# Pooled attention and a routed FFN on one core: emission order from a list scheduler, attention in thirds, four weight buffers

## The chip, the cores and the metric

The kernel runs on one core of one Trainium2 chip. A core has five engines with an instruction queue each: TensorE (PE, matmuls into PSUM; its weight loads are listed as PEld), VectorE (DVE), ScalarE (ACT), GpSimd (POOL) and SyncE (SP). Here GpSimd issues all loads,[...] and SyncE issues most stores. The metric is the device time of one execution in microseconds (us).

## The reference

Two parts follow each other. The first is attention over keys and values that are averaged over groups of 8 tokens; the second sends each token to the one of 8 experts whose embedding is nearest by cosine.

```python
batch, heads, seq, dim = 8, 8, 576, 64          # experts: 8, width 512 -> 1024 -> 512
k_p = k.reshape(B, H, 72, 8, D).mean(axis=3);  v_p = likewise
scores = q @ k_p.T / sqrt(D)
attn = exp(scores - max); attn /= sum(attn) + 1e-9
x = (attn @ v_p) as [4608 tokens, 512]
...
logits = normalized(x) @ normalized(expert_emb).T / tau
e = argmax(logits);  gate = softmax(logits)[e]
out = gate * (relu(x @ w1[e]) @ w2[e])
```

Which expert each token takes is known only on the chip, so the weights have to be fetched by a number that the kernel computes itself.

## The kernel before

The work is cut by batch: 576 tokens each. For a batch, attention makes x, transposed, in `xt_all`; then an FFN with one expert's weights gives the output rows. Several guesses keep the loads early: the mean of the pooled values is close to every token's x, so `guess_sum` and `guess` (L296 to L338) compute the expert of the whole batch from it long before x exists. Tokens that choose another expert would be done by a loop after the main part (L640); for that loop the kernel counts which experts occur (`count`, `present`).

The steps of a batch, with the lines that the prediction names:

- **Loads** (L540 to L597 for batches 0 and 1, `load_qkv` at L87 after that): k, q, v on GpSimd's queue.
- **VectorE preparation**: `kproc` adds and transposes the pooled k (L162 to L176), `qtr` transposes q in two halves of 288 columns (L185), `vadd` adds the values of a group (L194, L199).
- **Scores and exponentials**: `score` (L211, L217), four calls per batch, two PSUM tiles each; **PV**: `pv` (L231) in three units of 192 tokens; `xtr` (L243 to L248) divides by the sum and transposes into `xt_all`; `square` (L377) and `ssq` (L259, L263) give the lengths, whose square root `norm` takes on GpSimd (L413).
- **Routing**: `route` (L269 to L287), then `prob` and `gate` make the factor of each token.
- **Weights**: `weigh` reads the guessed expert into a register and issues w1 (L103) and w2 (L108). There are three pairs of buffers, `held`, used in turn. If the expert is already in one of the other buffers, the load is left out by a condition and `copy_w` (L359 to L361) copies on VectorE.
- **FFN**: eight groups `hgrp` (L454, ReLU at L460), then output blocks `yblk` (L468, scaled by the gate at L479) and a half-width last block `ylast` (L491, L498); stores at L524.

PSUM is used as four tiles of two banks, all under the name `pa`, taken in the order of emission.

What sets the order around the change is a list written by hand. The start is a fixed sequence (`run(...)`, L591 to L604), with dummy matmuls (`fill`, L143) between its parts. After it each step of attention and routing has a due time, a fraction of a batch (L58 to L75), and is emitted between the FFN's steps when the FFN's share of work has come that far (L614 to L625). Each engine executes its own instructions in the order in which they were emitted, and waits by semaphores for what they need.

Of the kernel before, what the change touches and what calls it, by code (L numbers as in the profile page):

```python
# [10 lines left out]
FP32 = mybir.dt.float32  # L11
FP16 = mybir.dt.float16
BF16 = mybir.dt.bfloat16
I32 = mybir.dt.int32
# [10 lines left out]

@with_exitstack
def kernel(
# [21 lines left out]
    TH = T // 2  # L49
    HG = H // 2  # L50
    NC = 5
    HALF = S // 2
    tau = float(moe_tau)
# [5 lines left out]
    atp = ctx.enter_context(tc.tile_pool(name="atp", bufs=10))  # L59
    xp = ctx.enter_context(tc.tile_pool(name="xp", bufs=3))  # L60
    rt = ctx.enter_context(tc.tile_pool(name="rt", bufs=2))
    hp_ = ctx.enter_context(tc.tile_pool(name="hp", bufs=2))
    yp = ctx.enter_context(tc.tile_pool(name="yp", bufs=8))
    ps = ctx.enter_context(tc.tile_pool(name="ps", bufs=4, space=bass.MemoryType.PSUM))

    def psum():
        return ps.tile([128, 1024], FP32, name="pa")
# [19 lines left out]
    def load_qkv(b):  # L87
        qq, kk, vv = new_qkv(b)
        nc.gpsimd.dma_start(out=kk, in_=flat(k, b))
        nc.gpsimd.dma_start(out=qq, in_=flat(q, b))  # L90
        nc.gpsimd.dma_start(out=vv, in_=grouped(v, b))


    NW = 3
# [7 lines left out]
    def load_w1(w1, e_val, cond=None):  # L102
        nc.gpsimd.dma_start(  # L103
            out=w1, cond=cond,
            in_=moe_w1[ds(e_val, 1)].squeeze(0).rearrange("(p w) f -> p w f", w=4))

    def load_w2(w2, e_val, cond=None):
        nc.gpsimd.dma_start(  # L108
            out=w2, cond=cond,
            in_=moe_w2[ds(e_val, 1)].squeeze(0).rearrange(  # L110
                "(w p r) d -> p w r d", p=128, r=2))
# [14 lines left out]
    tie_n = const.tile([128, E], FP16)  # L126
# [6 lines left out]
    emb_h = const.tile([E, 2, DM], FP16)  # L133
# [5 lines left out]

    def fill(cols, n):  # L140

        for _ in range(n):
            nc.tensor.matmul(out=cols, lhsT=ones_m[:, 0:128],  # L143
                             rhs=ones_m[:, 0:cols.shape[-1]], start=True, stop=True)
# [9 lines left out]
    def attn_steps(b):  # L154
        st = {}
        steps = []

        def kproc():


            kk = loads[b][1].rearrange("p (m r d) -> p m r d", r=4, d=D)
            nc.vector.tensor_tensor(out=kk[:, :, 0:2], in0=kk[:, :, 0:2],  # L162
                                    in1=kk[:, :, 2:4], op=ALU.add)
            ks = att.tile([128, T // 4, D], FP16, name="ks")
            nc.vector.tensor_tensor(out=ks, in0=kk[:, :, 0], in1=kk[:, :, 1], op=ALU.add)
            k4 = att.tile([128, T // 4, 2, 2, 16], FP16, name="k4")
            nc.vector.transpose(out=k4.rearrange("p m w r i -> p (m w r i)"),
                                in_=ks.rearrange("p m d -> p (m d)"))
# [11 lines left out]
        def qtr(half):  # L180


            qq = loads[b][0].rearrange("p (t d) -> p t d", d=D)[:, ts(half, TH)]
            qT = att.tile([128, 2, 2, TH * 16], FP16, name="qT", bufs=4)
            nc.vector.transpose(  # L185
                out=qT.rearrange("p w r (t i) -> p t w r i", i=16),
                in_=qq.rearrange("p t (w r i) -> p t w r i", w=2, r=2))
            st['qT', half] = qT

        def vadd(level):  # L190
            vv = loads[b][2].rearrange("g h (r d) -> g h r d", d=D)
            n = POOL >> (level + 1)
            if level < 2:
# [3 lines left out]
            vpx = att.tile([G, H, D + 2], FP16, name="vpx")  # L197
            nc.vector.memset(vpx[:, :, D:D + 2], float(POOL) / XS)
            nc.vector.tensor_tensor(out=vpx[:, :, 0:D], in0=vv[:, :, 0], in1=vv[:, :, 1],  # L199
                                    op=ALU.add)  # L200
            st['vpx'] = vpx

        def score(half, r, nfill=0):

            qT, kT = st['qT', half], st['kT']
            pS = [psum(), psum()]
            fill(pS[0][:, 0:288], nfill)
            for w in range(2):
                for a in range(HG):
                    rows = ts(a, 32)  # L210
                    nc.tensor.matmul(  # L211
                        out=pS[a // 2][0:G, (a % 2) * 512:(a % 2) * 512 + HALF],
                        lhsT=kT[rows, w, r, :], rhs=qT[rows, w, r, :],
                        start=(w == 0), stop=(w == 1))
            for i in range(2):
                at = atp.tile([G, 2, HALF], FP16, name="at")
                nc.scalar.activation(  # L217
                    out=at, in_=pS[i][0:G].rearrange("g (a c) -> g a c", a=2)[:, :, 0:HALF],
                    func=AF.Exp, scale=escale)
                st['at', half, r, i] = at  # L220

        def pv(u):

            px = psum()
            st['px', u] = px
            for j in range(6):
                half, blk = divmod(6 * u + j, 9)
                for r in range(2):
                    c0 = (j // 3) * 512 + ((j % 3) * 2 + r) * 80
                    for a in range(HG):  # L230
                        nc.tensor.matmul(  # L231
                            out=px[ts(a, 32), c0:c0 + D + 1],
                            lhsT=st['at', half, r, a // 2][:, a % 2, ts(blk, 32)],
# [3 lines left out]
        def xtr(u):  # L237


# [4 lines left out]
            x_sb = xp.tile([128, 2, 6, D], FP16, name="x_sb")  # L244
            nc.vector.tensor_tensor(  # L245
                out=x_sb, in0=pxv[:, :, :, 0:D],
                in1=rc.unsqueeze(3).to_broadcast([128, 2, 6, D]), op=ALU.mult)
            nc.vector.transpose(  # L248
                out=xt_all[:, b].rearrange("p w (t l) -> p t w l", l=32)[:, ts(u, 6)],
                in_=x_sb.rearrange("p b j d -> p (b j d)").rearrange(  # L250
                    "p (t l w) -> p t w l", w=4, l=32))

        def ssq():

            pq = psum()
            for c in (4, 0, 1, 2, 3):
                for w in range(4):
                    for rows in token_rows(c):
                        nc.tensor.matmul(out=pq[rows, c:c + 1],  # L259
                                         lhsT=st['sq'][:, w, cols(c)], rhs=ones_b,  # L260
                                         start=(w == 0), stop=(w == 3))
            st['ssq'] = rt.tile([128, NC], FP32, name="ssq")
            nc.vector.tensor_copy(out=st['ssq'], in_=pq[:, 0:NC])  # L263

        def route(c0, n, nfill=0):

            pl = psum()
            fill(pl[:, 512:704], nfill)
            nc.tensor.matmul(out=pl[:, 0:n * E], lhsT=ones_m[:, 0:128],  # L269
                             rhs=tie_l[:, 0:n * E], start=True, stop=False)  # L270
            for c in [n - 1, *range(n - 1)]:
                for w in range(4):
                    for rows in token_rows(c0 + c):
                        nc.tensor.matmul(out=pl[rows, ts(c, E)],  # L274
                                         lhsT=xt_all[:, b, w, cols(c0 + c)],
                                         rhs=enT[:, w, :],
                                         start=False, stop=(c == max(n - 2, 0) and w == 3))
            plv = pl[:, 0:n * E].rearrange("p (c e) -> p c e", e=E)
            if 'lg' not in st:
                st['lg'] = rt.tile([128, NC, E], FP32, name="lg")  # L280
                st['lmax'] = rt.tile([128, NC], FP32, name="lmax")
            cs = ds(c0, n)
            lmax = st['lmax'][:, cs]
            bc = lmax.unsqueeze(2).to_broadcast([128, n, E])
            nc.vector.tensor_reduce(out=lmax, in_=plv, axis=AX.X, op=ALU.max)
            nc.vector.tensor_tensor(out=oh_all[:, b, cs], in0=plv, in1=bc, op=ALU.is_ge)
            nc.vector.tensor_tensor(out=st['lg'][:, cs], in0=plv, in1=bc, op=ALU.subtract)  # L287

        def count(cs, pc):
            nc.tensor.matmul(out=pc[:, 0:E], lhsT=ones_m[:, 0:128], rhs=tie_n,  # L290
                             start=True, stop=False)
            for c in cs:
                nc.tensor.matmul(out=pc[:, 0:E], lhsT=ones_m[:, 0:128],
                                 rhs=oh_all[:, b, c], start=False, stop=(c == cs[-1]))

        def guess_sum():  # L296

            pm = psum()
            for h in range(H):
                nc.tensor.matmul(out=pm[ts(h % 2, 64), h // 2:h // 2 + 1],  # L300
                                 lhsT=st['vpx'][:, h, 0:D], rhs=ones_m[0:G, 0:1],
                                 start=True, stop=True)
            xb = rt.tile([128, 4, 128], FP16, name="xb")
            (nc.scalar.copy if b < 2 else nc.vector.tensor_copy)(
                out=xb, in_=pm[:, 0:4].unsqueeze(2).to_broadcast([128, 4, 128]))
            st['xb'] = xb

        def guess():


            pg = psum()
            for w in range(4):
                nc.tensor.matmul(out=pg[:, 0:E], lhsT=st['xb'][:, w], rhs=enN[:, w, :],
                                 start=(w == 0), stop=(w == 3))
            mx = rt.tile([128, E], FP32, name="mx")
            nc.vector.max(out=mx, in_=pg[:, 0:E])
            ix = rt.tile([128, E], U32, name="ix")
            nc.vector.max_index(out=ix, in_max=mx, in_values=pg[:, 0:E])
            ixf = rt.tile([128, 1], FP32, name="ixf")
            nc.vector.tensor_copy(out=ixf, in_=ix[:, 0:1])  # L320
# [3 lines left out]
            if b == 0:  # L324
                nc.vector.tensor_copy(out=own[:, 0:1], in_=ixf[0:1])
                return
# [380 lines left out]
```

The softmax here doesn't subtract the row's maximum and nothing guards it: scores larger than these inputs give would overflow.

## Time and profile before

| | |
|---|---|
| median of 3 runs | 234.39 us (233.79 to 235.03) |
| span of the profiled execution | 235.1 us |
| PE busy | 189.9 us, 81% |
| DVE busy | 148.8 us, 63% |
| ACT busy | 124.6 us, 53% |
| POOL busy | 37.5 us, 16% |
| moved by DMA | 36.67 MB, mean 156 GB/s |
| loads (software queue) | 26.75 MB, 63.0% of 16 engines |
| stores (hardware queue) | 8.86 MB, 11.4% |

Busy is the time in which the engine had an instruction in work; matmuls are pipelined, so a busy PE is not PE at its peak. The granted clock is the share of TensorE's full speed that it was allowed. Idle time is put down to what came last before the instruction. The page gives shares over the whole span; a table by stage says where they lie. "L454" is line 454 of the kernel; "pa<-xt_all,w" is what the instruction writes and reads.

### The profile page before, as it was taken

The page shows a single profiled execution, that of the slowest core. Times are in us where ns is not written, and L with a number is a line of the kernel's source. Part 1 is how long each engine was busy: PE and PEld are TensorE (multiplying, and loading weights), DVE is VectorE, ACT ScalarE, POOL GpSimd, SP SyncE. Part 2 cuts the span into 40 slices and gives each one's busy share as a digit, 9 for nine tenths or more (in the row PEclk, how much of TensorE's full clock was granted, in tenths as well). Part 3 has the DMA queues.
Part 4 walks back from the last instruction along what each step waited for, and adds up shares of the span by engine and source line. Part 5 has one row for each costly group of instructions (what it writes and reads, how often), then busy time and mean ns, then how long its engine had stood idle before and what let it go on. Part 6 is the DMA issues. An engine that isn't in the chain of part 4 may idle for free. (4 is left out here: it accounts for less than half of the span.)

```text
span 235.1 us, 6832 instructions
## 1 busy us (share of the span) xinstructions
PE 189.9 (81%) x2862; PEld 117.4 (50%) x2863; DVE 148.8 (63%) x391; ACT 124.6 (53%) x212; POOL 37.5 (16%) x59
## 2 busy tenths in 40 slices
PE   0038999880799959999999999969999997999900
PEld 0024466340466446655674576446654764586300
DVE  3967983794068994599669948971489679131200
ACT  3045269180186464756795487536665775554300
POOL 7306033200230003201320032002200200010000
PEclk9999999995599995999999999985899999999995
DMA  5997999999989078899999999964499400140240
GB/s 88 196 183 117 206 214 209 202 213 230 250 170 165 5 158 210 149 206 177 216 233 220 212 212 234 237 136 148 84 198 182 154 13 3 43 153 9 75 129 3
DMA packets 18242, 36.67 MB, mean 156 GB/s; under 512 B 2456, under 2 KB 8088, under 8 KB 17440
## 3 DMA queue, kind: packets, MB, share of 16 engines
q0 software_dynamic: 12752, 26.75, 63.0%
q1 hardware_dynamic: 5116, 8.86, 11.4%
q10 hardware_dynamic: 340, 0.59, 0.8%
q8 instruction: 23, 0.38, 0.6%
q14 instruction: 11, 0.09, 0.1%
HBM read 61.88 MB, written 9.44 MB: 303 GB/s over the span
## 5 line engine op out<-in xcount | busy, mean ns | idle before, releaser
L454 PE MATMUL pa<-xt_all,w 128*128 128x288 f16 x512 | 78.3, 305 | 11.2 <-DMA w<-in_moe_w_dram 10.6
L454 PEld LDWEIGHTS <-w 128*128 128x128 f16 x512 | 49.4, 103 | 30.1 <-DMA w<-in_moe_w_dram 10.9
L460 ACT ACTIVATE hT<-pa 128x576 f16<-128x576 f32 x64 | 41.5, 648 | 36.6 <-PE pa L454 36.6
L468 PE MATMUL pa<-w,hT 128*128 128x512 f16 x256 | 58.6, 379 | 0.2 <-ACT hT L460 0.2
L217 ACT ACTIVATE at<-pa 72x576 f16<-72x576 f32 x64 | 37.7, 643 | 12.7 <-PE pa L211 11.6
L468 PEld LDWEIGHTS <-hT 128*128 128x128 f16 x256 | 24.0, 98 | 27.2 <-ACT hT L460 1.4
L377 ACT ACTIVATE sq<-xt_all 128x768 bf16<-128x768 f16 x24 | 20.2, 843 | 32.3 <-DVE xt_all L248 28.0
L211 PE MATMUL pa<-qT,kT 32*72 32x288 f16 x256 | 16.6, 326 | 12.7 <-DVE qT L185 11.4
L479 ACT ACTIVATE y_sb<-pa,gm 128x512 f32<-128x512 f32 x30 | 18.9, 678 | 11.5 <-PE pa L468 11.5
L248 DVE STREAM_TRANSPOSE xt_all<-x_sb 128x768 f16<-128x768 f16 x24 | 23.5, 979 | 0.8
L245 DVE TENSOR_TENSOR x_sb<-pa,rc 128x768 f16<-128x768 f32 x24 | 23.0, 957 | 0.8
L413 POOL TENSOR_TENSOR ssq<-ssq,half_c 128x5 f32<-128x5 f32 x8 | 10.4, 1304 | 78.1 <-DVE ssq L263 78.0
L185 DVE STREAM_TRANSPOSE qT<-qq 128x1152 f16<-128x1152 f16 x16 | 21.2, 1356 | 1.1 <-DMA qq<-in_q_dram 1.1
L231 PEld LDWEIGHTS <-at 72*32 72x32 f16 x1152 | 12.0, 99 | 11.4 <-issue 10.7
L231 PE MATMUL pa<-vpx,at 72*32 72x65 f16 x1152 | 15.2, 201 | 3.0 <-issue 1.4
L194 DVE TENSOR_TENSOR vv<-vv 72x2048 f16<-72x2048 f16 (+1 forms) x16 | 15.0, 936 | 1.2 <-DMA vv<-in_v_dram 1.1
L211 PEld LDWEIGHTS <-kT 32*72 32x72 f16 x256 | 6.3, 115 | 17.5 <-DVE kT L176 9.8
L243 DVE RECIPROCAL rc<-pa 128x12 f32<-128x12 f32 x24 | 5.4, 226 | 11.7 <-PE pa L231 11.3
L103 POOL DMA_DIRECT2D w<-in_moe_w_dram x8 | 3.6, 452 | 44.3 <-DVEq L359 22.4
L263 DVE COPY ssq<-pa 128x5 f32<-128x5 f32 x8 | 1.3, 159 | 12.0 <-PE pa L259 12.0
L498 ACT ACTIVATE y_sb<-pa,gm 64x256 f32<-64x256 f32 x16 | 7.4, 466 | 2.3 <-PE pa L491 2.1
L491 PE MATMUL pa<-w,hT 128*64 128x256 f16 x128 | 8.5, 276 | 0.0
(102 smaller groups left out, 156.2 us busy)
## 6 DMA issues: line engine op xcount, KB each, us to landing
w<-in_moe_w_dram POOLq DMA_DIRECT2D x16, 1024.0 KB, 13.6
out_dram<-y_sb SPq DMA_DIRECT2D x30, 256.0 KB
kk<-in_k_dram POOLq DMA_DIRECT2D x8, 576.0 KB, 7.8
vv<-in_v_dram POOLq DMA_DIRECT2D x8, 576.0 KB, 15.8
qq<-in_q_dram POOLq DMA_DIRECT2D x7, 576.0 KB, 14.8
out_dram<-y_sb SPq DMA_DIRECT2D x15, 64.0 KB
qq<-in_q_dram POOLq DMA_DIRECT2D x2, 288.0 KB, 8.1
out_dram<-y_sb ACTq DMA_DIRECT2D x2, 256.0 KB
```

The lines of the kernel that those rows point to most:

```text
L185: nc.vector.transpose(out=qT.rearrange("p w r (t i) -> p t w r i", i=16), in_=qq.rearrange("p t (w r i) -> p t w r i", w=2, r=2))
L194: nc.vector.tensor_tensor(out=vv[:, :, 0:n], in0=vv[:, :, 0:n], in1=vv[:, :, n:2 * n], op=ALU.add)
L211: nc.tensor.matmul(out=pS[a // 2][0:G, (a % 2) * 512:(a % 2) * 512 + HALF], lhsT=kT[rows, w, r, :], rhs=qT[rows, w, r, :], start=(w == 0), ...
L217: nc.scalar.activation(out=at, in_=pS[i][0:G].rearrange("g (a c) -> g a c", a=2)[:, :, 0:HALF], func=AF.Exp, scale=escale)
L231: nc.tensor.matmul(out=px[ts(a, 32), c0:c0 + D + 1], lhsT=st['at', half, r, a // 2][:, a % 2, ts(blk, 32)], rhs=st['vpx'][:, 2 * a + r, 0: ...
L245: nc.vector.tensor_tensor(out=x_sb, in0=pxv[:, :, :, 0:D], in1=rc.unsqueeze(3).to_broadcast([128, 2, 6, D]), op=ALU.mult)
L248: nc.vector.transpose(out=xt_all[:, b].rearrange("p w (t l) -> p t w l", l=32)[:, ts(u, 6)], in_=x_sb.rearrange("p b j d -> p (b j d)").re ...
L377: nc.scalar.activation(out=st['sq'][:, :, cs], in_=xt_all[:, b, :, cs], func=AF.Square)
L454: nc.tensor.matmul(out=ph[:, half * 512:half * 512 + HALF], lhsT=w1v[:, kk, w // 2, w % 2, :], rhs=xt()[:, kk, ts(half, HALF)], start=(kk ...
L460: nc.scalar.activation(out=dst, in_=src, func=AF.Relu)
L468: nc.tensor.matmul(out=py, lhsT=st['hT', w // 4][:, (w // 2) % 2, w % 2, ts(c, 128)], rhs=w2[:, w // 2, w % 2, :], start=(w == 0), stop=(w ...
L479: nc.scalar.activation(out=y_sb, in_=py, func=AF.Copy, scale=g)
```

## The change

The order by hand is replaced by a planner that runs when the kernel is built. Every step is declared with its engine, an estimated duration, the steps it comes after, a priority, the PSUM tiles it takes and frees, and for a load the time on the DMA. `Plan.run` then steps through a model of the machine: it takes, engine by engine, the step that can start first (with a small window in which priority decides), assigns PSUM slots by what is free in the model, counts the DMA as one stream, and emits. Beside the order, these things change:

- attention works in three units of 192 tokens throughout (q transposes, scores, exponentials), where scores had halves of 288;
- four pairs of weight buffers for three; an expert that sits in the buffer whose turn it is needs neither load nor copy;
- the loads of batch 0 come as v, k, q, and v's sum for batch 0 is made on PE by matmuls with the identity; the loads are put into one sequence, in which w1, v1, q1, w2 of batch 0 are followed by w1 of batch 1, ahead of batch 2's inputs;
- the first two FFN groups of batch 0 start on the first half of the tokens;
- no dummy matmuls; one count of the experts at the end for one per batch; the cast of the mean (`xb`) always on ScalarE; one buffer for each half of hT for two;
- the copy of weights lies under one outer condition, and is declared independent of the conditional load, of which only one takes place.

```diff
+class Plan:
+    def step(self, eng, us, emit, after=(), pri=0.0, tiles=0, frees=(), dma=0.0, seq=None):
...
+    def run(self):
...
+            for eng, can in best.items():
+                first = min(c[0] for c in can)
+                best[eng] = min((c for c in can if c[0] <= first + NEAR.get(eng, 0.0)),
+                                key=lambda c: c[1])
+            t, _, o = min(best.values(), key=lambda c: c[:2])
...
+            o['emit']()
...
+            if o['dma']:
+                rings = max(rings, o['issued'] + 0.4) + o['dma']
+                o['end'] = rings + 1.2
...
-    hp_ = ctx.enter_context(tc.tile_pool(name="hp", bufs=2))
+    hp_ = ctx.enter_context(tc.tile_pool(name="hp", bufs=1))
...
-    NW = 3
+    NW = 4
...
+        def v_sum():
+            st['pv'] = psum()
+            for r in range(POOL):
+                nc.tensor.matmul(out=st['pv'][0:G, 0:H * D], lhsT=ident_h[0:G, 0:G],
+                                 rhs=loads[b][2][:, :, ts(r, D)],
+                                 start=(r == 0), stop=(r == POOL - 1))
...
+        for u in range(NU):
+            step(f's{u}', 'PE', 0.42, lambda u=u: score(u),
+                 ['kT', f'q{u}', (f'pv{u}', b - 1)], b - 10, tiles=2)
...
+            step(f'pv{u}', 'PE', 0.5, lambda u=u: pv(u), ['v', f'e{u}0', f'e{u}1'],
+                 b - 10, tiles=1)
...
+        step('root', 'POOL', 1.3, root, ['len_'], -1)
...
+        if b:
+            step('copy', 'DVE', 1.0, copy_w,
+                 ['eb', ('lw2', b - 1), ('y', b - NW)], b - 0.6, seq=('lw2', b))
...
+        load_v(0, [start])
+        load_k(0)
...
+        load_q(0, (1, 2))
...
+        load_k(1)
...
+        load_expert(0, 0)
+        load_v(1)
+        load_q(1)
+        load_expert(0, 1)
+        load_expert(1, 0)
+        load_batch(2)
+        load_expert(1, 1)
+        load_expert(2)
+        load_batch(3)
+        load_batch(4)
+        for b in range(3, B):
+            load_expert(b)
+            if b + 2 < B:
+                load_batch(b + 2)
```

## The prediction

> **What bounds the kernel now.** I read the time slices first, then a table by stage, then the waits, then the timeline at the points where TensorE (PE) stands still. In the slices each digit is the busy tenth of 5.9 us:
>
> ```profile
> PE   0038999880799959999999999969999997999900
> DVE  3967983794068994599669948971489679131200
> PEclk9999999995599995999999999985899999999995
> DMA  5997999999989078899999999964499400140240
> ```
>
> PE is the engine to keep busy: from slice 4 on it is nearly full. It is empty for about three slices at the start, in slice 9 (53 to 59 us) and after 223 us; and where it was interrupted, the granted clock falls to half. DMA is full for the first 70 us, then has holes. The table by stage (span, PE, PEld, DVE, ACT, POOL busy, then clock, DMA share, GB/s) gives sizes:
>
> ```profile
> 0.00:28.45 28.45, 12.35 (x234) 6.96 (x236) 20.25 (x57) 9.65 (x16) 10.37 (x22) 1.00 0.89 157
> 28.45:52.00 23.55, 22.02 (x362) 13.86 (x358) 17.25 (x46) 15.03 (x26) 5.39 (x6) 1.00 1.13 207
> 52.00:60.16 8.16, 0.00 (x0) 0.00 (x0) 3.42 (x8) 0.56 (x2) 0.00 (x0) 0.62 1.08 233
> 60.16:82.00 21.84, 21.64 (x316) 12.78 (x316) 14.45 (x38) 12.33 (x21) 3.83 (x7) 0.91 0.70 143
> 82.00:90.00 8.00, 5.57 (x87) 4.10 (x87) 7.61 (x15) 4.54 (x8) 0.58 (x2) 0.88 0.75 169
> 90.00:154.80 64.80, 63.97 (x1022) 39.91 (x1019) 49.76 (x128) 43.66 (x75) 12.34 (x16) 0.96 1.03 207
> 154.80:170.00 15.20, 13.34 (x169) 8.25 (x168) 5.78 (x22) 7.45 (x13) 2.53 (x3) 0.66 0.49 122
> 170.00:205.00 35.00, 33.28 (x520) 20.12 (x517) 26.25 (x63) 22.22 (x39) 1.28 (x3) 1.00 0.43 96
> 205.00:223.46 18.46, 17.73 (x171) 11.40 (x167) 4.02 (x20) 9.12 (x16) 1.17 (x1) 1.00 0.27 83
> 223.46:235.10 11.64, 0.00 (x0) 0.00 (x0) 0.00 (x0) 0.00 (x0) 0.00 (x0) 0.70 0.20 65
> ```
>
> So 235.1 us are 28.45 before the first FFN matmul, 195.0 from there to the last evacuation, and 11.6 of tail. Within the 195.0, PE is busy 177.6. Busy time times clock, row by row, is 22.0 + 19.7 + 4.9 + 61.4 + 8.8 + 33.3 + 17.7 = **168 us** of work at the full clock. The other 27 us are idle (17) and half clock (10). That, and the start, can be won. What ends these waits:
>
> ```profile
> PE pa L454 <- DMA w<-in_moe_w_dram: 10.6, 3, 8.2
> POOL w L103 <- DVEq L359: 22.4, 4, 7.7
> POOL ssq L413 <- DVE ssq L263: 78.0, 5, 17.7
> ```
>
> The long PE wait is for batch 1's weights. Its cause lies on GpSimd's in-order queue, as the timeline shows: weights are issued at 19.31 for batch 0 and only at 45.19 for batch 1, behind two whole batches of q, k, v:
>
> ```profile
> 19.31 0.54 POOL L103 DMA_DIRECT2D w<-in_moe_w_dram  x1 [11.37 <-DVE rc L243]
> 45.19 0.57 POOL L103 DMA_DIRECT2D w<-in_moe_w_dram  x1 [7.71 <-DVEq L359]
> 60.17 2.10 PE L454 MATMUL pa<-xt_all,w 128*128 128x288 f16 x8 [8.24 <-DMA w<-in_moe_w_dram]
> 63.38 1.20 POOL L413 TENSOR_TENSOR ssq<-ssq,half_c 128x5 f32<-128x5 f32 x1 [16.74 <-DVE ssq L263]
> 64.55 0.59 POOL L89 DMA_DIRECT2D kk<-in_k_dram  x1
> ```
>
> The last two lines show the same disease: the square root of L413 holds the queue for 16.7 us and the next k load leaves only after it, so the DMA has nothing to do around 76 to 82 us.
>
> **The skill.** "TensorE: Matmul & The Clock Gate", Part 1, says that the array starts at half clock and is released after some 3.4 us of activity, and that idle windows throttle it again. The trace agrees: the dummy matmuls at 24 us start 0.43 us apart and later four come in 0.80 us (0.20 each), and both the wait at 52 and the broken stretch at 82 to 90 are followed by a row of half clock. The same page, Part 1, Architectural detail, has VectorE, ScalarE and GpSimd as strict FIFOs; the 16.74 above is that. "DMA: Bandwidth & Descriptors", Issuing engines are not separate DMA queues, says that all issuers share 16 engines; so stores compete with loads, which I count below.
>
> **The change, part by part.**
>
> *Start.* v goes first and its pooled sum is made by eight 512-wide matmuls, so that the expert is guessed early. k of batch 0 was issued first at 1.42 and used at 7.09; v, whose issue takes 0.88 instead of 0.71, should be there at 7.3. Then: eight cold matmuls 8 x 0.43 = 3.4; evacuation on ScalarE 0.6 (the 512-wide cast of L304 took 0.59); means 0.38; cast 0.59; guess 0.27; max, index, cast 0.6; register and issue 1.25 (index done 18.06, issue 19.31); hops between engines, five at about 0.1, 0.5. Sum: w1 is issued at 14.9, against 19.31. It needs 8.0 us (the shortest landing of a weight, which is this one: the ring was empty). It is again empty: 2.36 MB moved before 15 us in the trace of before, exactly v, k, q of batch 0 and k of batch 1. w1 lands at 23. x must be ready too: k at 10.3, k work 2.9, q third 0.95, scores and two exponentials 2.6, PV, scale and transpose 3.2 give 20.3 for the first third; VectorE then needs 2.2 per third, so the second is ready at 22.5, the third at 24.7. The first FFN matmuls need two thirds only. FFN starts at **23.3** instead of 28.45: 5.1 gained. The dummy matmuls that had warmed the array are gone: about 4 us at half clock, **2 lost**.
>
> *Batch 1's weights.* After w1 of batch 0 the ring takes v1, q1, w2, then w1 of batch 1: 0.59 + 0.59 + 1.05 + 1.05 MB at 205 GB/s is 16 us, so they are in at 39 to 40, w2 of batch 0 at 34. PE from 23.3 has FFN 0 (64 x 0.123 + 32 x 0.221 + 1.0 = 15.9, from the timeline's dense runs), router and lengths 1.5, attention of batch 1 about 3.5, cold 2: until about 46. The wait of 8.2 and the half clock after it (4.83 us at 0.58, 2.0) go: **10 gained**. q, k, v of batch 2 then are in at 48, w2 of batch 1 at 53, when PE wants it at about 54.
>
> *Four buffers.* The inputs give experts 7, 5, 5, 1, 7, 4, 3, 4 (the reference evaluated on the fixed inputs). Batches 2 and 7 copy within three batches as now; batch 4 finds expert 7 in its own buffer, so that load falls away: 2.1 MB, or at the queue's 63.0% of 235 us for 26.75 MB, 11.6 us of DMA. And no load waits for a copy or the FFN before it; the wait of POOL for L359 goes. This is room on the DMA, not PE time: inputs then cost 136 us and stores 3.6 per batch. Walking the ring, batch 3's weights land at 89 to 94, when PE wants them at 88; I allow up to 3 us there. Batch 5's land at 130, batch 6's at 157, when PE wants them at 140 and 160: covered.
>
> *Order from a list scheduler.* Attention runs ahead when PE would wait. It could remove the rest of the idle time (17 - 8.2 = about 9) and of the half clock (10 - 2 = 8). I don't give it all: a model's durations are not the chip's, and a FIFO that is a microsecond early or late leaves holes. I leave **8** of these 17: the 3 for batch 3, 1 for the third x, 4 for small holes and a dip. The lower end is 2, the upper 17, as now.
>
> *Smaller edits.* Counting once instead of per batch takes away some 0.25 us of PE for seven batches, **1.7 gained**. Scores in 192 instead of 288 columns: 48 matmuls per batch for 32, columns the same; a call of eight lasts 0.38 in the dense timeline, 1.5 per batch, and I put 1.3 to 1.9 for the new form: nothing. Exponentials: 8 x 643 ns = 5.1 per batch become 6 of 768 elements, for which L377's 843 ns gives 5.1: nothing. q transposes gain a fixed cost, 3 x 0.95 for 2 x 1.36, +0.14 of VectorE per batch, and xb's 0.69 moves to ScalarE; VectorE stays at about 17 and ScalarE at 16 per batch beside PE's 20. One hT instead of two: ReLU of the next batch must wait for PE's last read, which is ahead of its own matmul in PE's queue anyway. Nothing.
>
> **Sum.** 23.3 + 168 - 1.7 + 2 + 8 = 199.6 for the last matmul, + 11.6 of tail (no edit touches it) = 211.2; the profiled execution was 0.7 longer than the median, so **210.5**.
>
> **Rivals.**
> - *The scheduler's order fits the chip almost exactly.* Half clock and holes shrink to 2: 204.5. For it: 90 to 154.8 shows that 64.8 us can hold 63.97 of PE. Against: ScalarE and VectorE at 80% each leave little slack. 0.15.
> - *The FIFOs bite again.* Start and batch 1 gain, but the square root or a load that waits for a late VectorE holds GpSimd's queue again, batch 3 or 5 waits, and the 17 stay: 219.5. For it: the root is still on GpSimd between loads, and 63.38 shows what that did. Against: one transfer fewer and a free buffer. 0.22.
> - *The order misfits: slower.* VectorE's queue holds a copy or a transpose early, everything queued behind it waits, and PE loses 3 to 4 us per batch at half clock after each: 8 x 4 on top of 211 is 243. For it: one FIFO order over five engines, fixed before the run. Against: the order is one of dependences, with priorities, and PE has 20 us per batch to hide 17. 0.08.
> - The forecast: 0.55.
>
> **Range.** From 203, a full realisation with a start one microsecond better, to 222, the second rival with a late batch 3. Faster by over 0.5%: 0.90; within: 0.02; slower: 0.08.
>
> **What would show it.** w1 issued near 15 and the first FFN matmul near 23; batch 1's FFN near 46 with no wait of several microseconds; eight pairs of weight issues of which three (batches 2, 4, 7) take only some 0.05 us each; PE's last matmul near 200; tail unchanged; half clock only in the first FFN and perhaps once more. Wrong if x, not w1, sets the start, if batch 3's weights come well after 90, or if idle PE time after 46 us exceeds 10.

## The result, and the profile after

The changed kernel takes **222.12 us** (median of 4, 221.62 to 224.27) against 234.09 (233.73 to 235.03) for the kernel before on the same chip: ratio 0.950 (95% interval 0.943 to 0.957). A second set of 6 executions gave 222.24. So the direction was right, and half of the forecast gain came: 12 us where 23.6 were forecast. Some executions of any kernel here run 1 to 4% longer at a lower granted clock; the ratios, and the times in the table of experiments, leave them out, but the profiled execution was one of them for the kernel before and for the seven experiments marked with a star.

The slices of the changed kernel, 5.5 us each, to be laid beside those of before:

```profile
PE   0436699999959999976999998897999999999910
DVE  2158977478977879979598977984988551021130
PEclk9999999999999999995599999999999999999985
DMA  3999995899999969999899999985422230240150
```

The empty slice at 53 to 59 us is gone. PE is interrupted in slice 11 (60 to 66 us) and in slices 17 and 18 (93 to 104), counted from 0. Only the latter cost clock: two digits of 5, in slices 18 and 19, where four stood before the tail. The table by stage (span, PE, PEld, DVE, ACT, POOL busy with counts, clock, DMA share, GB/s):

```profile
0.00:25.61 25.61, 10.07 (x221) 6.00 (x222) 13.94 (x55) 8.52 (x14) 7.61 (x19) 1.00 0.88 152
25.61:60.50 34.89, 34.48 (x490) 22.86 (x490) 26.76 (x78) 22.85 (x36) 8.04 (x13) 1.00 0.99 185
60.50:65.50 5.00, 2.75 (x39) 1.23 (x40) 4.02 (x4) 2.04 (x3) 2.03 (x3) 1.00 1.16 223
65.50:95.00 29.50, 28.65 (x529) 17.52 (x521) 25.04 (x65) 21.52 (x33) 4.59 (x8) 1.00 0.99 208
95.00:101.00 6.00, 3.02 (x74) 2.21 (x74) 4.66 (x10) 3.35 (x6) 0.86 (x1) 0.89 1.12 239
101.00:110.00 9.00, 9.00 (x150) 5.81 (x150) 5.95 (x15) 5.72 (x8) 2.30 (x3) 0.51 0.95 194
110.00:152.50 42.50, 38.95 (x673) 24.48 (x672) 34.71 (x88) 30.06 (x48) 5.78 (x8) 1.00 0.99 206
152.50:209.35 56.85, 56.53 (x783) 36.04 (x781) 26.17 (x71) 34.50 (x56) 3.61 (x5) 1.00 0.26 73
```

The idle time of PE is the second column less the third. It lies in three places: the wait at 61 us (2.25), the hole at 95 to 101 (2.98), and small holes in 110 to 152.5 (3.55). The row of 101 to 110 is full but at clock 0.51: 4.4 us lost there. After 152.5 next to nothing is lost (0.3). I keep one account for all kernels, from slices of 5 us between the first FFN matmul and the last output matmul: idle is span less busy, half clock is busy times (1 - clock), work is what remains.

| | first FFN | idle | half clock | work | last matmul | tail | span |
|---|---|---|---|---|---|---|---|
| before | 28.5 | 16.8 | 10.2 | 167.3 | 222.7 | 12.4 | 235.1 |
| forecast | 23.3 | 8.0 together | | 168.3 | 199.6 | 11.6 | 211.2 |
| after | 25.6 | 10.3 | 4.7 | 168.7 | 209.35 | 10.25 | 219.6 |

(Forecast work is 168 less 1.7 plus 2 for the cold array; its 168 and 11.6 are cut at the last evacuation, 0.7 us after the last matmul. In the records the clock reads 1.00 while the array is cold at the start, when an FFN matmul takes 0.26 us instead of 0.13, so that the cold time stands in "work" in all rows. The profiled execution of the kernel before took 236.73, 2.3 us above its median, and its row holds that much more.)

Three points of the trace carry the rest. First the weights and the first uses of them, as the timeline shows (start, duration, engine, line, what; in brackets the idle time before it and its releaser):

```profile
14.39 0.17 DVE L477 MAX8 mx<-pa 128x8 f32<-128x8 f32 x1 [1.64 <-PE pa L471]
16.08 0.55 POOL L201 DMA_DIRECT2D w<-in_moe_w_dram  x1 [9.78 <-DVE k L283]
24.48 0.98 DVE L376 STREAM_TRANSPOSE xt_all<-x_sb 128x768 f16<-128x768 f16 x1
25.61 3.15 PE L596 MATMUL pa<-xt_all,w 128*128 128x288 f16 x12 [1.32 <-DVE rc L368]
31.71 1.20 POOL L403 TENSOR_TENSOR ssq<-ssq,half_c 128x5 f32<-128x5 f32 x1 [12.90 <-DVE ssq L400]
36.39 0.59 POOL L201 DMA_DIRECT2D w<-in_moe_w_dram  x1 [3.48 <-DVE lg L432]
57.17 0.05 POOL L201 DMA_DIRECT2D w<-in_moe_w_dram  x1 [0.95 <-DMA w<-in_moe_w_dram]
63.46 1.90 PE L615 MATMUL pa<-w,hT 128*128 128x512 f16 x8 [2.25 <-DMA w<-in_moe_w_dram]
```

The first FFN waits for x, not for weights: w1 landed 8.0 us after its issue, at 24.1, and the second third of x, which the first matmuls read, is transposed only at 25.46. (The profile names the reciprocal of L368, which stands right behind that transpose in VectorE's queue.) Batch 1's w1 is issued at 36.39; batch 2's, already in a buffer, costs 0.05. Batch 1's w2 is late by 2.25 us. Second, the hole, in the timelines of PE and ScalarE around it:

```profile
87.61 0.53 PE L340 MATMUL pa<-qT,kT 32*72 32x192 f16 x16
93.29 0.53 PE L340 MATMUL pa<-qT,kT 32*72 32x192 f16 x16
96.20 0.96 ACT L646 ACTIVATE y_sb<-pa,gm 64x256 f32<-64x256 f32 x2 [0.31 <-PE pa L637]
97.18 0.81 ACT L347 ACTIVATE at<-pa 72x768 f16<-72x768 f32 x1
98.04 0.55 PE L358 MATMUL pa<-vpx,at 72*32 72x65 f16 x46 [0.62 <-ACT at L347]
100.95 1.12 PE L596 MATMUL pa<-xt_all,w 128*128 128x288 f16 x4 [2.36 <-DVE xt_all L376]
```

It is one chain: batch 3's third scores at 93.29, 5.7 us after its second; its last exponentials at 97.18, behind evacuations of output; PV, the scaling and the transpose on VectorE; and then FFN 3, at half clock. The third scores had their q transposed by 86.2 us. What held them is settled in the last group of experiments.

### The profile page after: what moved, and what is told of

The parts are those of the page before. It is cut to its first block, busy times and chain, and to the rows that moved or that the text cites. A ratio compares the mean times of both kernels' runs of the same rounds, so it can differ in the third digit from the quotient of the medians.

```text
span 219.6 us, 6958 instructions
## 1 busy us (share of the span) xinstructions
PE 183.6 (84%) x2937; PEld 116.1 (53%) x2938; DVE 142.7 (65%) x388; ACT 129.3 (59%) x203; POOL 34.8 (16%) x59
## 4 chain that ended last, share of the span: by engine, by line
PE 65%; DMA 14%; ACT 7%; DVE 6%; issue 2%; POOL 1%; POOLq 0%
PE pa L596 25%; PE pa L615 23%; DMA w<-in_moe_w_dram 11%; PE pa L358 4%; DMA vv<-in_v_dram 3%; PE pa L340 3%; PE pa L637 3%; PE pa L413 2%; PE pa L394 2%; ACT at L347 2%; ACT y_sb L625 2%; PE pa L324 2%; DVE xt_all L376 1%; DVE x_sb L370 1%; ACT xb L463 1%
## 5 line engine op out<-in xcount | busy, mean ns | idle before, releaser
L596 PE MATMUL pa<-xt_all,w 128*128 128x288 f16 x512 | 75.3, 301 | 5.1 <-DVE xt_all L376 2.4
L615 PE MATMUL pa<-w,hT 128*128 128x512 f16 x256 | 59.3, 379 | 4.5 <-DMA w<-in_moe_w_dram 2.2
L347 ACT ACTIVATE at<-pa 72x768 f16<-72x768 f32 x48 | 36.8, 800 | 14.3 <-PE pa L340 14.1
L403 POOL TENSOR_TENSOR ssq<-ssq,half_c 128x5 f32<-128x5 f32 x8 | 9.5, 1188 | 95.2 <-DVE ssq L400 76.4
L301 DVE STREAM_TRANSPOSE qT<-qq 128x768 f16<-128x768 f16 x24 | 21.8, 949 | 0.0
L340 PE MATMUL pa<-qT,kT 32*72 32x192 f16 x384 | 14.3, 272 | 3.4 <-DVE qT L301 3.4
L368 DVE RECIPROCAL rc<-pa 128x12 f32<-128x12 f32 x24 | 5.3, 222 | 16.0 <-PE pa L358 15.5
L314 DVE TENSOR_TENSOR vv<-vv 72x2048 f16<-72x2048 f16 (+1 forms) x14 | 13.2, 939 | 1.9 <-DMA vv<-in_v_dram 1.6
L340 PEld LDWEIGHTS <-kT 32*72 32x72 f16 x384 | 8.6, 118 | 10.5 <-issue 4.6
L423 DVE TENSOR_REDUCE lmax<-pa 128x5 f32<-128x40 f32 x8 | 1.6, 200 | 15.1 <-PE pa L413 15.0
L201 POOL DMA_DIRECT2D w<-in_moe_w_dram x8 | 3.0, 372 | 47.9 <-DMA w<-in_moe_w_dram 25.6
L271 DVE TENSOR_TENSOR kk<-kk 128x1152 f16<-128x1152 f16 x8 | 6.0, 746 | 5.5 <-DMA kk<-in_k_dram 4.5
## 6 DMA issues: line engine op xcount, KB each, us to landing
vv<-in_v_dram POOLq DMA_DIRECT2D x8, 576.0 KB, 25.6
kk<-in_k_dram POOLq DMA_DIRECT2D x8, 576.0 KB, 10.3
```

The costliest lines, as they stand in the source:

```text
L301: nc.vector.transpose(out=qT.rearrange("p w r (t i) -> p t w r i", i=16), in_=qq.rearrange("p t (w r i) -> p t w r i", w=2, r=2))
L340: nc.tensor.matmul(out=pS[a // 2][0:G, ds(a % 2 * 512 + r * SU, SU)], lhsT=kT[ts(a, 32), w, r, :], rhs=qT[ts(a, 32), w, r, :], start=(w == ...
L347: nc.scalar.activation(out=at.rearrange("g a r c -> g a (r c)"), func=AF.Exp, scale=escale, in_=st['pS', u][p][0:G].rearrange("g (a c) -> ...
L596: nc.tensor.matmul(out=st['ph', w][:, half * 512:half * 512 + HALF], lhsT=w1v[:, kk, w // 2, w % 2, :], rhs=xt()[:, kk, ts(half, HALF)], s ...
L615: nc.tensor.matmul(out=py, lhsT=st['hT', w // 4][:, (w // 2) % 2, w % 2, ts(c, 128)], rhs=w2[:, w // 2, w % 2, :], start=(w == 0), stop=(w ...
```

## The experiments

All are edits of the changed kernel, except one. The time is the median; in brackets stands how many executions it is of, where some were left out. The ratio is to the kernel before, on the same chip; first FFN, idle and half clock are those of the profiled execution. The first four ran on one chip, those from "fewer loads" to "exponentials first" on a second, the rest on a third. The kernel before had a median of 235.21 on the second and of 234.1 to 234.6 on the others, so that across chips the ratios compare better than the times.

| | time | ratio, 95% | first FFN | idle | half clock |
|---|---|---|---|---|---|
| root late * | 220.55 (1 of 4; all: 224.70) | none from one | 25.8 | 11.7 | 7.2 |
| v1 first | 223.77 | 0.952 to 0.966 | 25.9 | 10.0 | 6.1 |
| both | 222.50 | 0.940 to 0.960 | 25.7 | 10.0 | 5.6 |
| warm * | 225.66 (3 of 4) | 0.954 to 0.974 | 27.4 | 14.4 | 8.6 |
| early sum for batch 1 | 223.53 | 0.947 to 0.969 | 30.0 | 8.1 | 3.1 |
| hole filled | 224.60 | 0.951 to 0.974 | 25.7 | 10.6 | 5.7 |
| order with three buffers * | 228.46 (2 of 4) | 0.964 to 0.998 | 25.5 | 18.2 | 7.9 |
| before, four buffers * | 229.10 (9 of 17) | 0.975 to 0.984 | 29.3 | 13.7 | 7.5 |
| fewer loads * | 220.90 (4 of 5) | 0.937 to 0.948 | 25.6 | 10.7 | 5.8 |
| fewer transposes | 224.36 | 0.953 to 0.964 | 25.8 | 11.6 | 4.9 |
| early sum for batch 3 | 224.83 (4 of 5) | 0.953 to 0.964 | 26.0 | 10.3 | 6.9 |
| exponentials first | 220.25 | 0.934 to 0.942 | 25.6 | 10.2 | 6.0 |
| pair held * | 220.43 (5 of 6) | 0.940 to 0.954 | 26.0 | 11.1 | 5.9 |
| pair held, exponentials first | 218.61 | 0.930 to 0.944 | 25.9 | 9.3 | 2.6 |
| changed kernel again | 222.24 | 0.947 to 0.959 | 26.1 | 10.4 | 4.8 |
| all loads lighter * | 212.43 (2 of 6; all: 215.41) | 0.902 to 0.920 | 25.9 | 6.3 | 5.0 |

**Batch 1's weights and the start.** The DMA moved only 63 GB/s at 35 to 40 us, and batch 1's w1 was issued at 36.39, 18 us after the load ahead of it (18.05). My first theory was that this hole, handed on through the pipeline, was the missing gain. Three edits tried to close it:

```diff
-        step('root', 'POOL', 1.3, root, ['len_'], -1)
+        step('root', 'POOL', 1.3, root, ['len_'], -1, seq=None if b else ('lw1', 1))
```

> The square root of batch 0 is emitted behind the load of batch 1's w1; nothing else is asked. Theory A (batch 1's guess itself is late, since v of batch 1 lands behind w1 of batch 0): the w1 load leaves where it left, 36 us, and the time stays at 222 within 1. Theory B (the square root at the head of GpSimd's queue is what holds the load): it leaves some 3 us earlier and the time falls by 2 to 4, to 218 to 220. Theory C (loads don't matter, the order misfits on VectorE and PE): 222.

Batch 1's w1 went at 35.65 instead of 36.39. The root isn't what holds it.

```diff
-        load_k(1)
+        load_v(1)
...
-        load_v(1)
+        load_k(1)
```

> v of batch 1 is loaded ahead of its k, so before w1 of batch 0; the square root stays ahead of batch 1's w1. Theory A: batch 1's expert is known before the FFN starts, the load leaves as soon as the square root lets it (33 to 34 us, 2 to 3 earlier), the wait of 2.2 us at 61 us goes and part of the hole at 95 to 101; 217 to 220. Theory B: the same queue head still holds it, less than 1 gained, 221 to 222. Theory C: 222.

It is issued at 35.08, and the time is unchanged or a little worse. Both edits together:

> Both edits: v of batch 1 ahead of its k, and batch 0's square root behind batch 1's w1. If the late weights of batch 1 are what moved every later transfer, the hole in the DMA at 34 to 39 us closes, w1 of batch 1 leaves near 20 us, w2 of batch 1 lands some 4 to 5 us earlier than 63, the wait at 61 and the hole at 95 to 110 (3 us idle, 4 of half clock) mostly go: 213 to 217. Theory C: 222.

It is issued at 35.09. v of batch 1 is there at about 19, but its second addition is executed at 27.59, behind batch 0's x in VectorE's queue; the guess follows at 32 to 34. In between, its mean and its guess stand on PE behind batch 0's router and lengths (30.18 and 32.31). So the issue was set by VectorE's queue first and by PE's after it, and the next edit took the sum off VectorE:

```diff
-            attention(b, early=(b == 0))
+            attention(b, early=(b < 2))
```

> On top of the two edits before, the pooled sum of v is made on PE for batch 1 too (as for batch 0), so that batch 1's expert no longer waits behind VectorE's work on x of batch 0. Theory A (the DMA hole at 34 to 39 us and the late w2 of batch 1 at 63 us are what costs): w1 of batch 1 leaves before 28 us, w2 lands at 58 to 60, PE's wait at 61 (2.2 us) goes and attention of batch 3 comes 3 to 5 us earlier, so that part of the hole at 95 to 110 goes too: 215 to 219. Theory E (PE is busy without a break from 25 to 60 us anyway, and the hole at 95 is made by attention of batch 3 on ScalarE and VectorE, not by the DMA): 220 to 223.

With the two other edits in, w1 of batch 1 is issued at 28.72, the DMA moves 211 GB/s from 30 to 40, and the wait at 61 us is gone. The time is 223.53 all the same, though idle and half clock fell to 11: the first FFN came 4.4 us later, because batch 1's sum and its evacuation went ahead of batch 0's x. What the earlier weights won (3.8) the later start took away, so this run alone doesn't refute the theory. Two things speak against it. In the changed kernel PE is busy 34.48 of the 34.89 us to 60.5, so that the DMA hole can cost it no more than what comes later; and the kernel with fewer loads, below, has the start at 25.6 and no wait at 61, and wins only 1 to 2.5 us.

The cold array was tried with dummy matmuls of 512 columns (6 ahead of the first scores, 5 in PV, 4 ahead of the first FFN group):

> Dummy matmuls of 512 columns are put back: 6 ahead of the first scores, 2 and 3 ahead of the second and third PV, 4 ahead of the first FFN group of batch 0. Theory D (the first 9 us of the FFN run at half clock, 4.4 us lost): matmuls of the first FFN run 0.12 us apart from about 27 us on; since the time to the end follows PE, 2.5 to 4 us faster, 218 to 220. If early PE time is not on the path, because batch 1's weights set the pace until 63 us anyway: same within 1.

The array is warm, eight FFN matmuls take 1.14 instead of 2.10, and the first output block begins 1.5 us earlier (38.19 against 39.69). Batch 1's weights are issued 0.8 us earlier (w1 at 35.59), since PE computes the guess at 32.62 instead of 33.56, and w2 with them: PE's wait for it ends at 62.63 instead of 63.46. So of the 1.5 us 0.8 are left at that point, and the kernel is no faster: 225.66. Where it loses the rest isn't shown; in the profiled execution, the longest of the four, the eight matmuls behind the wait run at half clock (3.53 us instead of 1.90).

**The hole at 95 us.** Eight dummies before one group of FFN 3, to keep the array awake:

```diff
+            for _ in range(8 if (b, w, half) == (3, 0, 1) else 0):
+                nc.tensor.matmul(out=st['ph', w][:, 512:1024], lhsT=ones_m[:, 0:128],
+                                 rhs=ones_m, start=True, stop=True)
```

> Eight dummy matmuls of 512 columns go ahead of the first matmuls that wait for the third x of batch 3, into the half of the PSUM tile that they write over. If the hole before them (2.4 us idle at 98.6 to 101) is what throttles the clock to half for the 9 us that follow, the clock stays full and 3 to 4 us are gained: 218 to 219, and the hole itself stays. If the clock falls for another reason, or falls elsewhere instead: 222.

The clock in 100 to 110 is 0.91 instead of about 0.5, but 0.75 in 110 to 120, and there are dips near 55 and 155. Half clock went elsewhere; nothing was gained.

```diff
-            attention(b, early=(b == 0))
+            attention(b, early=(b in (0, 3)))
```

> Batch 3's sum of v is also made on PE, as batch 0's is, so VectorE has 2.3 us less before batch 3's third x. If VectorE is what delays that x, the hole of 3 us near 95 us and the half clock after it (4 us) go, for 1 us more of PE work: 216 to 219. If single holes are only replaced by others, as in the earlier runs: 221 to 224.

The order changes, a wait of 2.5 us between 105 and 110 takes the place of the hole, and the time is worse.

```diff
-                ... exp(u, p), [f's{u}'], b - 5,
+                ... exp(u, p), [f's{u}'], b - 30,
```

> The exponentials get a priority ahead of all evacuations on ScalarE. If ScalarE's queue order makes the hole near 95 us, where the last exponentials stand behind output evacuations, the hole shrinks by 1 to 2 us, and with it the half clock after it: 217 to 220. If the hole comes from the chain's length or from VectorE: 221 to 224, with the hole where it was.

220.25, 2 us better by the times and about 3 by the ratios (0.938 against 0.950 and 0.953), and not in the way that I expected. The hole is still there (2.63 us before 101.57). What is gained lies in 115 to 155 us: PE is busy 38.24 of these 40 against 36.92 and 36.70 in the two profiles of the changed kernel.

```profile
115.00:155.00 40.00, 38.24 (x696) 24.49 (x694) 34.44 (x83) 29.14 (x47) 5.84 (x9) 1.00 0.96 199
```

**Buffers and order apart.** The changed kernel with NW = 3, and the kernel before with NW = 4 (one hT buffer and seven output buffers to make room, and the code that picks the copy adapted):

> Three weight buffers under the new order, which stays word for word the same; batch 4 has to load its expert again (2.1 MB, 11 us of DMA) and batch 3's and later loads wait for the FFN three batches earlier. If the fourth buffer carries much of the gain: 227 to 232, by waits for the weights of batch 5 or 6 near 120 to 160 us. If the order carries it: 222 to 225.

> The kernel before with four weight buffers alone (room for it comes from one hT buffer and one output buffer less); its order is unchanged. If the buffers carry the gain: 226 to 230. If the order does: 231 to 235; the wait for batch 1's weights at 52 us stays in both cases, and the one at 155 us may go (2 us and some half clock).

With three buffers batch 4's weights are loaded again (issued at 93.47 and 95.23). v of batch 6, issued behind them at 95.97, is in only at about 134.9, and PE's longest wait in the profiled execution becomes the one for its sum:

```profile
PE pa L457 <- DVE vpx L318: 8.9, 1, 8.9
```

In the kernel before, the fourth buffer makes that load free, and of three waits of PE for weights it leaves the one for batch 1's, as it was:

```profile
120.67 0.04 POOL L103 DMA_DIRECT2D w<-in_moe_w_dram  x1 [2.96 <-DMA w<-in_moe_w_dram]
PE pa L456 <- DMA w<-in_moe_w_dram: 8.3, 1, 8.3
```

What goes is above all the wait for batch 5's weights, which ended at 156.66 (1.83 us), with the half clock behind it: from 152 to 172 us PE is busy 19.98 at full clock, where it was 18.14 at 0.74. So buffers alone are worth 2.1% (1.6 to 2.5), the rest of the change with three buffers 1.9% (0.2 to 3.6), both together 4.7 to 5.0%. The two add up, with perhaps a per cent of joint gain that the intervals don't separate. What the order is worth without the edits that came with it was not tried.

**What load is left.** Two kernels leave work out to see what bounds the middle: one has FFN 1 and 3 use the buffers of batches 0 and 2, with no load of their own; one takes old transposes of q from batch 2 on. A third does both and has the exponentials first. The core of the two edits:

```diff
+    USE = {1: 0, 3: 2}
+    def buf(b):
+        return held[USE.get(b, b) % NW]
...
+            if b >= 2:
+                st['qT', u] = turned[b % 2, u]
+                return
```

> The loads of batch 1's and batch 3's weights are left out (4.2 MB of 24.65 MB); their FFNs use the weights of batches 0 and 2, so the output rows of these two batches are not the reference's. If the DMA (mean share 1.0 from 46 to 146 us) is what keeps the pipeline tight, the loads run up to 20 us earlier, the hole at 95 us shrinks, idle and half clock fall from 15 to under 8 and the time to 213 to 216. If the order and the latency of the attention chain on VectorE and ScalarE make the holes, the time stays within 2 us of 222, although the wait near 61 us goes.

> From batch 2 on the transposes of q are left out (the scores use the queries of the batch two before), which takes 3 x 0.94 = 2.8 us per batch, 17 us in all, off VectorE; the output of batches 2 to 7 is not the reference's. If VectorE's queue ahead of the attention makes the holes, PE's idle and half-clock time between 60 and 152 us falls by 5 or more, and the time to 214 to 218. If DMA or ScalarE make them, the time stays within 2 us of 222.

> Loads of batch 1's and 3's weights left out, q transposes left out from batch 2, exponentials first (the output of most batches is not the reference's). If the load on DMA and VectorE together makes the holes: idle and half clock under 9, 212 to 215. If the order and the PSUM tiles make them: 218 to 221.

With 4.2 MB less to load the time is 220.90, 1.3 us under the changed kernel (by the ratios 0.7 to 1.1%, 1.7 to 2.5 us), and the hole stays, 2.8 us long. With 17 us less on VectorE it is 224.36, not better at all: the hole shrinks and one of 3.6 us opens behind it, where the next batch's scores wait. Neither alone is the bound. All three together give 212.43 from two executions, 215.41 over all six (211.87 to 220.59): 5 to 8 us better than the exponentials alone, and idle time is 6.3. A caution goes with the group: less declared work also gives the planner another order, so part of each difference is the order's.

**PSUM.** PSUM is four tiles. Scores need two at once, everything else one. The planner takes the step that can start first, so each tile that comes free goes to a step that needs one, and a score step waits until two happen to be free. Between 87.6 and 93.3 PE executed two PV units, the mean, the guess and 16 matmuls of output blocks; the third scores, with q ready and a better priority than the output blocks, came after them. The hole belongs to the order and not to the chip's durations: in the planner's own reckoning, which is a model and no measurement, PE also waits 2.9 us at that place for the same x. The edit makes other tile users of lower priority wait while this one step is ready but for its tiles:

```diff
+            pairs = [(self.ready(o, False), o) for o in left
+                     if any(o is self.named.get(n) for n in (('s2', 3),))]
...
+                can = [c for c in best['PE'] if not c[2]['tiles'] or c[1] <= top['pri']
+                       or c[0] < when]
```

> The planner holds back requests for PSUM tiles while the third score call of batch 3 waits for its two tiles. If PSUM is what delays that call (ready at 86 us, executed at 93.3), it runs before 91, the hole of 3 us at 95 to 101 shrinks to under 1.5, no half clock follows, and the time is 216 to 219. If PSUM is not the cause the call stays near 93; if it is but another hole opens, as in the runs before, the hole at 95 goes and the time is 221 to 224.

> The pair of tiles held for the third score call of batches 2 and 3, and the exponentials ahead of the evacuations on ScalarE; the planner's own clock ends 3 us earlier than for the changed kernel. If PSUM and ScalarE's order together make the holes in the middle: idle and half clock fall from 15 to 9 or 10, time 215 to 218, faster than the changed kernel. If holes only move: 220 to 222.

> The changed kernel as it is, on the chip of the other three runs: 221 to 223.5, with the hole near 95 to 101 again where it was.

Held for batch 3 alone, the call starts at 91.15 instead of 93.63 (the changed kernel in the same set), and the hole of 95 to 101 is gone: FFN 3 begins at 100.15 with no wait before it for its third x.

```profile
91.15 0.84 PE L351 MATMUL pa<-qT,kT 32*72 32x192 f16 x12
100.15 1.65 PE L607 MATMUL pa<-xt_all,w 128*128 128x288 f16 x12
```

So the tiles held the call, and the call made the hole. A smaller pause of 1.3 us stands within the scores themselves, for which the profile shows no releaser, with about 1.6 us of half clock. Busy times clock in 85 to 115 is 26.1 against 21.7. The time is 220.43, 1.8 us better, but the executions of the two overlap (219.10 to 222.39 against 221.26 to 223.94). In 115 to 155 the profile has 33.3 against 36.7; it is that of the longest execution of the six (223.39), so that this loss can't be put down to the edit. The kernel with both edits, and then the changed kernel again, in the table by stage:

```profile
85.00:115.00 30.00, 28.39 (x473) 16.77 (x470) 25.05 (x56) 20.15 (x32) 5.69 (x10) 0.94 1.01 204
115.00:155.00 40.00, 38.17 (x713) 24.82 (x710) 34.80 (x92) 29.99 (x48) 6.96 (x11) 1.00 0.98 207
```

```profile
85.00:115.00 30.00, 26.10 (x506) 15.85 (x505) 24.26 (x64) 19.48 (x30) 3.83 (x8) 0.83 1.03 217
115.00:155.00 40.00, 36.70 (x645) 22.81 (x645) 32.34 (x77) 27.42 (x44) 5.81 (x9) 1.00 0.96 200
```

Busy times clock is 26.7 against 21.7 in the first row, and 38.2 against 36.7 in the second: 6.5 us. Before 85 us the edited kernel is 3 us behind (its wait for batch 1's w2 is 3.0 instead of 2.0, and brings half clock with it). The rest, 3.5, is the difference: **218.61** against 222.24, and no execution of one (216.79 to 219.97) reaches into those of the other (221.26 to 223.94). This version beats both kernels. How much of its time is the pair's is not shown: the exponentials alone have a ratio of 0.938 (0.934 to 0.942), both edits 0.937 (0.930 to 0.944), and the 1.6 us between their medians were measured on two chips. The trace alone tells them apart: in 85 to 115 us the exponentials by themselves have a busy times clock of 21.9, like the changed kernel, and in 115 to 155 us the same 38.2 as both edits.

## Why the prediction was wrong in size

The direction held; the range missed by 0.12 us, and that it came so close is no merit: its upper end stood for the rival with the square root and a late batch 3, which is not what happened. The account: the span was 219.6 instead of 211.2. Of these 8.4 us, 2.3 are the start, 7.0 idle time and half clock (15.0 instead of 8), 0.4 work, and -1.35 the tail. Another 3.2 us lie between span and time.

- **The failed step: "I leave 8 of these 17".** Measured: 15. The 8 were "the 3 for batch 3, 1 for the third x, 4 for small holes and a dip". The 3 at batch 3 were right in size and place (2.98 at 95 to 101) but wrong in cause: weights were there, batch 3's third x was not. The half clock after it, 4.4 us, alone exceeds the 4 that were to hold all small holes and the dip, though the profile of before shows such a dip after a hole (clock 0.66 in 154.8 to 170). The small holes were 3.55 in 110 to 152.5, the wait for batch 1's w2, put at nothing, 2.25, and scattered pieces 1.6. What makes the hole at 95 is, by the experiments, the planner's treatment of two-tile steps; the small holes shrink by 1.3 to 1.5 us with ScalarE's order (both edits: 3.6 us won back). A joint load on DMA and VectorE may hold the rest (5 to 8 us more when both are lightened, little or nothing when one is), but those runs changed the order too. I had named "a FIFO that is early or late"; PSUM I never looked at, though the diff shows "tiles=2" in the score step.
- **"FFN starts at 23.3".** It was 25.61, and x set it, not w1, the case that I had named as making the forecast wrong. w1 was issued at 16.08 (14.9 forecast), since v was used from 8.78, not 7.3. k was used from 11.50, not 10.3; and its transpose on VectorE came at 15.27, behind the guess in the same queue, where I had let the two run beside each other: VectorE stood idle for 1.64 us until the guess's matmul was done, with the transpose waiting behind. (The parts of the sum for the first third add up to 19.95, too, not to 20.3.)
- **Cold array: 2.** Measured about 4: 24 FFN matmuls at 0.26 instead of 0.13 are 3.2, and the 32 after them and the router's 24 at 4.60 and 0.90 instead of 4.08 and 0.78 add 0.6; some small ones the rest. I took the Trainium skill's 3.4 us of activity ("TensorE: Matmul & The Clock Gate", Part 1) for the length of the cold stretch; here it lasted from 25.6 to about 34, with PE counted busy throughout. Yet the experiment with dummies shows that little of it was on the path: of 1.5 us won, 0.8 were left at the wait of 61 us, and the kernel was no faster.
- **Batch 1: "10 gained".** The mechanism was right, the times were not. w1 was issued at 36.39, and FFN 1 began at 50.85 rather than 46, without a wait; w2, forecast in at 53, came at 63.4 and cost 2.25. The walk of the ring took the order of the loads and left out that batch 1's w1 needs a guess, and the guess needs VectorE, which was busy with batch 0's x, and then PE.
- **Four buffers: "room on the DMA, not PE time".** Wrong: 2.1% by themselves in the kernel before, about 5 us, and about 3% within the new order (0.981 against 0.950 and 0.953). Room on the DMA became PE time, because loads behind the saved one come in earlier and PE waits for some of them: batch 5's weights in the kernel before, batch 6's v in the new order. Three of eight issue pairs cost 0.05, as forecast, and the weights of batches 3, 5 and 6 cost PE nothing.
- **Edits at nothing, and the count.** Work 168.7 against 168.3: fits in sum; since the cold stretch took 2 more than forecast, the rest took some 1.6 less, and which edit did that was not tried. The tail was 10.25, not 11.6 ("no edit touches it"); counted from the last matmul it was 12.4 before, so that it is 2.1 shorter. What shortened it was not tried.
- **"0.7 longer than the median".** A misreading. The reported time is 1.6 to 2.2 us above the span in all executions, and the profiled execution of before was 236.73 against a median of 234.39. The two nearly cancelled. For the changed kernel the span of 219.6 stands for 221.62, and 0.5 more to the median.
- **Rival "the FIFOs bite again", 219.5**, came nearest in time, but not by its cause: the root alone was not to blame, and batches 3 and 5 did not wait for weights. "Idle after 46 exceeds 10" stands at 9.95.

Left open: what the pair of tiles adds to the exponentials in time; which part of the 5 to 8 us is load and which the other order; and whether holding tiles for every batch would pay, which was not tried.

## What to carry to other kernels

When an order comes from a scheduler, look for requests of different sizes on one resource: who needs two tiles at once starves under a rule of "who can start first", and the hole appears microseconds later on another engine. Reckon with half clock behind a hole in TensorE: here 3 us of hole cost 4.4 more, while the wait of 2.25 us at 61 us cost none. And don't expect a closed hole to be paid out in full: one edit won 1 to 3 us or nothing, two together 3.6.

## What the hardware showed beyond the forecast

In the hole the granted clock fell at about 99.7 us and came back at 109.9, though PE was without a pause from 101: some 9 us of busy time at half clock. The Trainium skill ("TensorE: Matmul & The Clock Gate", Part 1) gives about 3.4 us of sustained activity for the release, and here it was over twice that, with the small matmuls of scores and PV (32x192 and 72x65) among the FFN's. For the throttling the same part names an idle window of about 3.4 us; here 0.6 and 2.4 us of idle time, with half a microsecond of PV between them, were enough.
